# Attention followed by a gated MLP on one core: weights converted in PSUM without POOL, layer norm's scaling on ACT, v's remainder on VectorE, and the first batch's product with v divided by the sums

## The chip, the core and the metric

The kernel runs on one core of one Trainium2 chip. The metric is the device time of one execution in microseconds (us). The engines are called as in the profile: PE (matrix products; PEld its weight loads), DVE (VectorE), ACT (ScalarE), POOL (GpSimd) and SP, which issues the DMAs.

## The reference

There are 4 batches of 768 tokens. Attention has 8 heads of 64; each token sees 8 global tokens and the last 96 tokens, with a bias that falls with the distance. Its output, 512 wide, goes through an MLP whose second half of hidden units is normalised, mixed over the tokens and multiplied with the first half.

```python
scores = scale * np.matmul(q, k.transpose(0, 1, 3, 2))
scores = np.where(keep, scores + bias[None], -1000000000.0)
scores = scores - np.max(scores, axis=-1, keepdims=True)
a = np.exp(scores)
a = a / (np.sum(a, axis=-1, keepdims=True) + 1e-09)
x = np.matmul(a, v)                       # then (batch, token, 512)
h = np.maximum(x @ w_in, 0.0)
u, v = h[..., :512], h[..., 512:]
v_n = (v - mean(v)) / np.sqrt(var(v) + 1e-06)
v_s = np.einsum('ts,bsd->btd', w_spatial, v_n) + b_spatial[None, :, None]
out = (u * v_s) @ w_out
```

The inputs q, k, v and w_spatial are fp32. The weights w_in and w_out come as 64-bit floats.

## The kernel before, in words

**Blocks.** A batch has 6 blocks of 128 tokens; n counts the 24 blocks of all batches. Block n needs only its own keys and those of the block before it, with the global keys copied over the first columns of the older one. For a block, `prep` loads q and k, `prep_v` loads v, `scores` makes the probabilities and `values` the product with v.

**Scores.** PE multiplies (L364 in batch 0, L367 in the others) into PSUM tiles of two heads. On DVE, L373 adds the bias and takes the row maximum; on ACT, L377 makes the exponentials and, by an accumulator, their sums `sm`. L259 and L260 (function `recip`, DVE) add 1e-9 to the sums of four heads and take the reciprocals `rc`; then L388 on POOL multiplies each head's probabilities with its reciprocal.

**Values.** PE transposes the probabilities (L421), ACT brings them out of PSUM, and PE multiplies with v (L430 in batch 0, L451 in the others). The result x is kept as two parts, a rounded `xth` (ACT) and a remainder `xtl` (DVE or POOL); L123 and L127 are the helpers that write any such pair. In batch 0 this is done on halves of 64 partitions straight out of PSUM. The branch for `folded(n)` exists but is not taken, since `CFG["fold"]` is empty: there the probabilities stay undivided, the reciprocals of all 8 heads are spread over 512 columns (`rows`, a buffer shared with the q input of later batches), transposed by PE and copied by ACT to `div` (shared with the k input), and the product with v is multiplied with them.

**Batch 0 and the rest.** Batch 0 multiplies q with k and probabilities with v in plain fp32. The other batches split q, k, v and the probabilities into a rounded part and a remainder; v's split is on POOL (L129 the rounded part, L123 the remainder), and the split q and k are copied by 12 DMAs a block (L300 to L303).

**Weights.** `split_weights` turns a 128x512 piece of 64-bit weights into a rounded part and a remainder. There are 8 pieces of w_in and 4 of w_out. One ACT operation (L222) makes the absolute values, six DVE operations (L223 to L228) assemble the fp32 number and its low part, ACT rounds (L50), and POOL subtracts and adds (L230, L231). All tiles are in SBUF. The fp32 spatial weights are split on ACT and POOL (`w_t_h`, `w_t_l`, 128x768, six of them).

**MLP.** `mlp_v` (L493 on PE) computes a block's second half of hidden units; ACT applies the relu, DVE takes mean and variance (L499, L500), POOL computes (var + 1e-6)^-0.5 (L501, L502), DVE scales (L503), and ACT and POOL split the result into `vnh` and `vnl`. `mlp_u` (L516) computes the first half for 256 tokens, `mlp_s` (L531) mixes over the tokens, and `mlp_o` (L549) multiplies with w_out. Each takes its PSUM tiles from the pool `ps_m`, which has two buffers.

**Order.** The lists `S` (batch 0) and `T` (the others) in `CFG` give the order of the steps in the program: P is `prep`, S `scores`, W `prep_v`, A `values`; V, U, G, O are the MLP steps with their lag in batches and their block; I and Q convert w_in and w_out, T the spatial weights. A scheduler with a timeline model then reorders the instructions of each engine. So each engine has one queue, worked off in order, and what stands in it is fixed before the run. The letters after `CFG` keys such as `vhi` name the engine of an operation: a for ACT, v for DVE, p for POOL.

Of the kernel before, what the change touches and what calls it, by code (L numbers as in the profile page):

```python
# [30 lines left out]
def attn_then_spatial_gating_kernel(  # L31
# [173 lines left out]
    def split_weights(src, hi, lo, key=None):  # L205
        w = src.shape[-1]
        if src.dtype == F32:
            st = work.tile([P, w], F32, name="wst", tag="u", bufs=3)
# [13 lines left out]
        nc.scalar.activation(m, upper.bitcast(F32), AF.Abs)  # L222
        nc.vector.tensor_scalar(out=c, in0=upper.bitcast(F32), scalar1=UPPER_MAX, scalar2=-UPPER_MAX, op0=ALU.min, op1=ALU.max)  # L223
        nc.vector.tensor_scalar(out=ai, in0=ci, scalar1=3, scalar2=0x3FFFFFFF, op0=ALU.logical_shift_left, op1=ALU.bitwise_and)
        nc.vector.scalar_tensor_tensor(out=ai, in0=ci, scalar=-0x40000000, in1=ai, op0=ALU.bitwise_and, op1=ALU.bitwise_or)
        nc.vector.scalar_tensor_tensor(out=a, in0=m, scalar=UPPER_MIN, in1=a, op0=ALU.is_ge, op1=ALU.mult)
        nc.vector.tensor_scalar(out=ci, in0=ai, scalar1=-0x800000, scalar2=None, op0=ALU.bitwise_and)
        nc.vector.scalar_tensor_tensor(out=m, in0=lower.bitcast(U32), scalar=2.0 ** -52, in1=c, op0=ALU.mult, op1=ALU.mult)  # L228
# [1 line left out]
        E("wsub").tensor_tensor(out=a, in0=a, in1=hi.bitcast(F32), op=ALU.subtract)  # L230
        E("wadd").tensor_tensor(out=lo, in0=a, in1=m, op=ALU.add)  # L231
# [26 lines left out]
    def recip(out, sums):
        nc.vector.tensor_scalar(out=out, in0=sums, scalar1=1e-9, scalar2=None, op0=ALU.add)  # L259
        nc.vector.reciprocal(out=out, in_=out)  # L260
# [80 lines left out]
    def scores(n, qq):  # L341
# [14 lines left out]
        rc = work.tile([P, H], F32, name="rc", bufs=2)
        W = P if i == 0 else 2 * P
        probs = []
        for g in range(NP):
# [8 lines left out]
            for j in range(2):  # L368
# [8 lines left out]
                nc.scalar.activation(pr, pr, AF.Exp, bias=mn[:, h:h + 1], scale=-1.0, accum_out=sm[:, h:h + 1])  # L377
# [109 lines left out]
    def mlp_v(b, i):  # L487
# [14 lines left out]
        nc.gpsimd.tensor_tensor(out=rs, in0=rs, in1=nhalf, op=ALU.pow)  # L502
        nc.vector.tensor_scalar(out=vr, in0=vr, scalar1=mv[:, 0:1], scalar2=rs, op0=ALU.subtract, op1=ALU.mult)  # L503
# [238 lines left out]
```

## Time and profile before

| | |
|---|---|
| median of 3 runs | 530.93 us (529.34 to 532.43) |
| profiled execution | 530.32 us |
| span of its instructions | 528.5 us |
| mean granted clock of PE | 0.970 |
| PE busy | 474.2 us (90%), weight loads 427.9 us (81%) |
| DVE busy | 350.6 us (66%), 972 instructions |
| POOL busy | 325.4 us (62%), 450 instructions |
| ACT busy | 301.9 us (57%), 800 instructions |

The span is 1.8 us shorter than the profiled execution's time. The busy times are sums over the whole span, and the stages differ, so a share says little about any one of them. A group of instructions is shown by line, engine, operation, written tile, read tiles, shape and count, with the busy time, the mean in ns, and the engine's idle time just before. In the timeline a row starts with the start and the duration in us. Chains and waits are inferred from semaphores.

### The profile page before, as it was taken

Reading aid. Unit: us, or ns where it says so; the run is one execution under the profiler, and the core shown is the slowest. Engines: PE = TensorE matmul, PEld = TensorE weight load, DVE = VectorE, ACT = ScalarE, POOL = GpSimd, SP = SyncE. Lnnn points to the kernel's source line nnn. Section 1 sums busy time; section 2 is a strip of 40 time slices with the busy share of each in tenths; the row PEclk is TensorE's granted clock in tenths of the full one; section 3 lists DMA queues with packets and bytes.
Section 4 is the critical chain, followed back from the end, with each engine's and each line's share of the span. In section 5 each row is a group of like instructions: output and inputs, shape, how many; then the busy total and the mean of one; then the engine's idle time right before and its main releaser. Section 6 shows DMA issues by size and latency. Waiting matters only on the chain.

```text
span 528.5 us, 9830 instructions
## 1 busy us (share of the span) xinstructions
PE 474.2 (90%) x3116; PEld 427.9 (81%) x3116; DVE 350.6 (66%) x972; ACT 301.9 (57%) x800; POOL 325.4 (62%) x450
## 2 busy tenths in 40 slices
PE   3757599898988999997989999989999999979994
PEld 2535489678977999986979899969989899869994
DVE  6899988869697585476785775767587856331210
ACT  3775478666666484666575575675475576431111
POOL 6999997866774753846662947644753757523320
PEclk9987789999999999999999999998999999989998
DMA  7993412961755755466655764655755760000002
GB/s 173 288 245 106 144 60 52 214 145 51 153 139 138 172 133 125 98 154 160 145 118 150 169 163 99 147 146 137 159 112 147 183 140 21 22 20 1 21 35 73
DMA packets 68269, 65.50 MB, mean 124 GB/s; under 512 B 6672, under 2 KB 49936, under 8 KB 68208
## 3 DMA queue, kind: packets, MB, share of 16 engines
q1 hardware_dynamic: 68208, 64.78, 49.9%
q8 instruction: 27, 0.44, 0.4%
q14 instruction: 34, 0.28, 0.2%
HBM read 29.76 MB, written 6.68 MB: 69 GB/s over the span
## 4 chain that ended last, share of the span: by engine, by line
PE 48%; DVE 17%; DMA 13%; SPq 8%; ACT 6%; issue 5%; POOL 2%; DVEq 0%; ACTq 0%; POOLq 0%
PE sps L531 13%; PE vps L493 8%; PE ups L516 8%; PE ops L549 7%; PE ops L451 4%; DVE pr L373 3%; PE pt L421 3%; DMA qkraw<-in_k_dram 3%; PE sp L367 3%; ACT pr L377 2%; DMA qkraw<-in_q_dram 2%; DMA kring<-qkraw 2%; SPq L303 2%; DVE qkraw L123 2%; SPq L300 2%
## 5 line engine op out<-in xcount | busy, mean ns | idle before, releaser
L388 POOL TENSOR_SCALAR pr<-pr,rc 128x256 f32<-128x256 f32 (+1 forms) x192 | 99.6, 537 | 23.4 <-DVE rc L260 9.1
L377 ACT ACTIVATE pr<-pr,mn 128x256 f32<-128x256 f32 (+1 forms) x192 | 92.2, 482 | 33.7 <-DVE mn L373 32.5
L421 PE MATMUL pt<-ident,pr 128*128 128x128 f32 x352 | 58.4, 280 | 14.7 <-POOL pr L388 11.6
L373 DVE CUSTOM_DVE_ANT_0 pr<-sp,bias 128x256 f32<-128x256 f32 (+1 forms) x192 | 68.1, 395 | 4.6 <-PE sp L364 1.4
L421 PEld LDWEIGHTS pt<-ident,pr 128*128 128x128 f32 x352 | 42.0, 143 | 23.9 <-POOL pr L388 16.5
L123 DVE TENSOR_TENSOR pth<-pt,pth 128x512 fp32r<-128x512 f32 (+1 forms) x72 | 46.0, 642 | 16.6 <-ACT pth L127 15.4
L535 POOL TENSOR_TENSOR g<-g,u 128x512 f32<-128x512 f32 x24 | 32.0, 1331 | 34.8 <-DVE g L533 34.7
L127 ACT ACTIVATE pth<-pt 128x512 fp32r<-128x512 f32 (+1 forms) x72 | 39.2, 558 | 23.6 <-PE pt L421 20.9
L123 POOL TENSOR_TENSOR xtl<-c,xth 128x256 fp32r<-128x256 f32 x36 | 27.3, 758 | 35.8 <-ACT xth L127 28.5
L123 POOL TENSOR_TENSOR vnl<-vr,vnh 128x512 fp32r<-128x512 f32 x24 | 31.9, 1332 | 27.6 <-ACT vnh L127 26.6
L531 PE MATMUL sps<-w_t_l,vnh 128*128 128x256 f32 x288 | 45.8, 286 | 0.0
L531 PE MATMUL sps<-w_t_h,vnh 128*128 128x256 f32 x288 | 44.9, 286 | 0.8 <-ACT u L517 0.5
L451 PE MATMUL ops<-pth,vring 128*128 128x256 f32 x264 | 41.8, 288 | 3.0 <-DVE pth L123 2.1
L461 DVE TENSOR_TENSOR c<-ops,c 64x256 f32<-64x256 f32 x72 | 30.3, 421 | 21.4 <-ACT c L50 16.6
L531 PE MATMUL sps<-w_t_h,vnl 128*128 128x256 f32 x288 | 44.4, 285 | 0.0
L364 PE MATMUL sp<-kring,q 128*128 128x256 f32 (+1 forms) x96 | 28.7, 450 | 16.8 <-DMA kring<-in_k_dram 9.9
L451 PEld LDWEIGHTS ops<-pth,vring 128*128 128x128 f32 x264 | 36.4, 192 | 5.2 <-DVE pth L123 2.8
L367 PE MATMUL sp<-kring,q 128*128 128x256 f32 (+1 forms) x144 | 38.3, 292 | 2.4 <-DMA q<-qkhi 1.2
L531 PEld LDWEIGHTS sps<-w_t_h,vnh 128*128 128x128 f32 x288 | 38.7, 191 | 1.6 <-ACT vnh L127 0.8
L531 PEld LDWEIGHTS sps<-w_t_l,vnh 128*128 128x128 f32 x288 | 39.0, 191 | 0.0
L533 DVE TENSOR_TENSOR g<-sps,b_bc 128x512 f32<-128x512 f32 x24 | 16.5, 686 | 33.8 <-PE sps L531 31.5
L531 PEld LDWEIGHTS sps<-w_t_h,vnl 128*128 128x128 f32 x288 | 38.6, 191 | 0.0
(115 smaller groups left out, 1204.4 us busy)
## 6 DMA issues: line engine op xcount, KB each, us to landing
q<-qkhi SPq DMA_DIRECT2D x72, 128.0 KB, 2.5
ql<-qkraw SPq DMA_DIRECT2D x72, 128.0 KB, 2.5
out_dram<-o SPq DMA_DIRECT2D x23, 256.0 KB, 2.6
qkraw<-in_q_dram SPq DMA_DIRECT2D x36, 128.0 KB, 3.0
qkraw<-in_k_dram SPq DMA_DIRECT2D x36, 128.0 KB, 2.9
raw<-in_v_dram SPq DMA_DIRECT2D x18, 256.0 KB, 3.2
kring<-qkhi SPq DMA_DIRECT2D x36, 128.0 KB, 2.5
kring<-qkraw SPq DMA_DIRECT2D x36, 128.0 KB, 2.5
```

Of the source, the lines that this page charges most:

```text
L123: e_lo.tensor_tensor(out=lo, in0=src, in1=hi.bitcast(F32), op=ALU.subtract)
L127: nc.scalar.activation(hi, src, AF.Copy)
L367: nc.tensor.matmul(sp[:, j], lhsT=a[:, g, j] if CFG["dup"] else a[:, h], rhs=kring[:, h, sl], start=(y == 0), stop=(y == 1))
L373: nc.vector.tensor_tensor_reduce(out=pr, in0=sp[:, j], in1=bt, scale=-scale, scalar=3e38, op0=ALU.add, op1=ALU.min, accum_out=mn[:, h:h + 1],)
L377: nc.scalar.activation(pr, pr, AF.Exp, bias=mn[:, h:h + 1], scale=-1.0, accum_out=sm[:, h:h + 1])
L388: nc.gpsimd.tensor_scalar(out=pr, in0=pr, scalar1=rc[:, h:h + 1], scalar2=1.0, op0=ALU.mult, op1=ALU.mult)
L421: nc.tensor.transpose(pt[:, c, j], probs[2 * g + j][:, c * P:(c + 1) * P], ident)
L451: nc.tensor.matmul(ops[:, j], lhsT=vring[:, order[c], g, 2 * j:2 * j + 2].rearrange("p x d -> p (x d)"), rhs=pth[:, 2 * c + j].rearrange(" ...
L493: nc.tensor.matmul(ps, lhsT=a[:, t, toks], rhs=w[:, t, FH:], start=(x == 0), stop=(x == len(passes) - 1))
L516: nc.tensor.matmul(ps[:, j], lhsT=w[:, t, f * P:(f + 1) * P], rhs=a[:, t], start=(x == 0), stop=(x == len(passes) - 1))
L531: nc.tensor.matmul(ps[:, j], lhsT=vn[b, s][x][:, f * P:(f + 1) * P], rhs=w[:, s, ts_], start=(y == 0), stop=(y == len(passes) - 1))
L549: nc.tensor.matmul(ps[:, cs], lhsT=a[:, f, x * P:(x + 1) * P], rhs=w[:, f, cs], start=(y == 0), stop=(y == len(passes) - 1))
```

## The change

Five things change, all by `CFG` and the code behind it.

- `wp`: `split_weights` keeps its working number `wx` in a PSUM tile of `ps_m`, computes in place, and does the last subtraction and sum on DVE. ACT's two operations stay.
- `fold` is `'0'`: batch 0 takes the folded branch. The 48 products on POOL go; per block come one `rows` copy on POOL, 4 transposes on PE, one `div` copy on ACT, 4 products on DVE (64x256), and the split of x on 128 partitions in two ACT and two DVE operations instead of four and four.
- `vhi`, `vlo`: v's rounded part moves from POOL to ACT, its remainder from POOL to DVE.
- `vrn`: the layer norm's scaling moves from DVE to ACT as scale and bias per row; POOL computes the bias, minus mean times scale, by two more operations on one column.
- `bias1`, `bias2`: the 16 scalings that make the bias tables move from POOL to ACT.

The sums now lie in two tiles whose second column holds 1e-9, and `recip` adds the pair with a reduction instead of adding a constant; in batch 0 it is called once per block.

```diff
-CFG = {... 'bias1': 'pppppppp', 'bias2': 'pppppppp', ... 'vhi': 'p', 'vlo': 'p', ... 'fold': '', ...}
+CFG = {... 'bias1': 'aaaaaaaa', 'bias2': 'aaaaaaaa', ... 'vhi': 'a', 'vlo': 'v', ... 'wp': 1, 'vrn': 'a', ... 'fold': '0', ...}
...
+        if CFG["wp"]:
+            x = ps_m.tile([P, w], F32, name="wx", tag="m")
+            xi = x.bitcast(I32)
+            a = work.tile([P, w], F32, name="wa", tag="vnl", bufs=6)
+            m = work.tile([P, w], F32, name="wm", tag="ev", bufs=nb("ev"))
+            ai = a.bitcast(I32)
+            nc.scalar.activation(m, upper.bitcast(F32), AF.Abs)
+            nc.vector.tensor_scalar(out=x, in0=upper.bitcast(F32), scalar1=UPPER_MAX, scalar2=-UPPER_MAX, op0=ALU.min, op1=ALU.max)
+            nc.vector.tensor_scalar(out=ai, in0=xi, scalar1=3, scalar2=0x3FFFFFFF, op0=ALU.logical_shift_left, op1=ALU.bitwise_and)
+            nc.vector.scalar_tensor_tensor(out=xi, in0=xi, scalar=-0x40000000, in1=ai, op0=ALU.bitwise_and, op1=ALU.bitwise_or)
+            nc.vector.scalar_tensor_tensor(out=x, in0=m, scalar=UPPER_MIN, in1=x, op0=ALU.is_ge, op1=ALU.mult)
+            nc.vector.tensor_scalar(out=ai, in0=xi, scalar1=-0x800000, scalar2=None, op0=ALU.bitwise_and)
+            nc.vector.scalar_tensor_tensor(out=m, in0=lower.bitcast(U32), scalar=2.0 ** -52, in1=a, op0=ALU.mult, op1=ALU.mult)
+            cp(E("whi"), hi, x)
+            nc.vector.tensor_tensor(out=x, in0=x, in1=hi.bitcast(F32), op=ALU.subtract)
+            nc.vector.tensor_tensor(out=lo, in0=x, in1=m, op=ALU.add)
+            return
...
+    sums = [pers.tile([P, H, 2], F32, name=f"sums{x}") for x in range(2)]
+    for x in range(2):
+        nc.vector.memset(sums[x], 1e-9)
     def recip(out, sums):
-        nc.vector.tensor_scalar(out=out, in0=sums, scalar1=1e-9, scalar2=None, op0=ALU.add)
+        nc.vector.tensor_reduce(out=out, in_=sums, op=ALU.add, axis=mybir.AxisListType.X)
         nc.vector.reciprocal(out=out, in_=out)
...
-        sm = work.tile([P, H], F32, name="sm", bufs=2)
+        sm = sums[n % 2]
...
-                nc.scalar.activation(pr, pr, AF.Exp, bias=mn[:, h:h + 1], scale=-1.0, accum_out=sm[:, h:h + 1])
+                nc.scalar.activation(pr, pr, AF.Exp, bias=mn[:, h:h + 1], scale=-1.0, accum_out=sm[:, h, 0:1])
...
-        nc.vector.tensor_scalar(out=vr, in0=vr, scalar1=mv[:, 0:1], scalar2=rs, op0=ALU.subtract, op1=ALU.mult)
+        if CFG["vrn"] == "a":
+            sh = work.tile([P, 1], F32, name="sh", bufs=2)
+            nc.gpsimd.tensor_tensor(out=sh, in0=mv[:, 0:1], in1=rs, op=ALU.mult)
+            nc.gpsimd.tensor_scalar(out=sh, in0=sh, scalar1=-1.0, scalar2=1.0, op0=ALU.mult, op1=ALU.mult)
+            nc.scalar.activation(vr, vr, AF.Identity, bias=sh, scale=rs)
+        else:
+            nc.vector.tensor_scalar(out=vr, in0=vr, scalar1=mv[:, 0:1], scalar2=rs, op0=ALU.subtract, op1=ALU.mult)
```

The scheduler makes a new order out of this on every engine. Three places follow; lines of the changed kernel are larger by 18 to 28.

On POOL, the beginning of batch 0 before: the probabilities' products (L388), the weights' subtraction and sum (L230, L231) and the spatial weights' remainders (L123) alternate.

```order
L388 TENSOR_SCALAR pr<-pr,rc 128x128 x4
L230 TENSOR_TENSOR wa<-wa,w_in_h 128x512
L388 TENSOR_SCALAR pr<-pr,rc 128x128 x4
L231 TENSOR_TENSOR w_in_l<-wa,wm 128x512
L265 TENSOR_SCALAR kring_114<-kg 128x4x32
L123 TENSOR_TENSOR w_t_l<-wst_493,w_t_h 128x768
L230 TENSOR_TENSOR wa<-wa,w_in_h 128x512
L388 TENSOR_SCALAR pr<-pr,rc 128x256 x4
L123 TENSOR_TENSOR w_t_l<-wst_497,w_t_h 128x768
```

The same place now, where `rows` are the spread reciprocals of a block:

```order
L54 TENSOR_SCALAR rows<-rc 128x512
L123 TENSOR_TENSOR w_t_l<-wst_479,w_t_h 128x768
L123 TENSOR_TENSOR w_t_l<-wst_483,w_t_h 128x768
L287 TENSOR_SCALAR kring_118<-kg 128x4x32
L123 TENSOR_TENSOR w_t_l<-wst_824,w_t_h 128x768
L123 TENSOR_TENSOR w_t_l<-wst_871,w_t_h 128x768
L54 TENSOR_SCALAR rows<-rc 128x512
```

Only the spatial weights' remainders, the global keys (`kg`) and the new copies are left there.

On DVE, the first two pieces of w_out before: the conversion runs through the six operations, with a remainder of x between.

```order
L223 TENSOR_SCALAR wc<-wst 128x512 x2
L259 TENSOR_SCALAR rc<-sm 128x4
L260 RECIPROCAL rc<-rc 128x4
L224 TENSOR_SCALAR wa<-wc 128x512 x2
L225 SCALAR_TENSOR_TENSOR wa<-wc,wa 128x512 x2
L226 SCALAR_TENSOR_TENSOR wa<-wm,wa 128x512 x2
L227 TENSOR_SCALAR wc<-wa 128x512
L123 TENSOR_TENSOR xtl<-ops,xth 64x2x128
```

The end of the same two pieces now. `wx` is the tile in PSUM, `xs` the divided product, and `qkraw` the input of batch 1's first block.

```order
L229 SCALAR_TENSOR_TENSOR wx<-wm,wx 128x512
L282 RECIPROCAL rc<-rc 128x8
L462 TENSOR_TENSOR xs<-ops,div 64x256
L229 SCALAR_TENSOR_TENSOR wx<-wm,wx 128x512
L462 TENSOR_TENSOR xs<-ops,div 64x256
L230 TENSOR_SCALAR wa<-wx 128x512 x2
L231 SCALAR_TENSOR_TENSOR wm<-wst,wa 128x512 x2
L233 TENSOR_TENSOR wx<-wx,w_out_h 128x512 x2
L234 TENSOR_TENSOR w_out_l<-wx,wm 128x512 x2
L123 TENSOR_TENSOR qkraw<-qkraw,qkhi 128x512 x2
L123 TENSOR_TENSOR xtl<-xs,xth 128x2x128 x2
```

Both pieces hold a buffer of `ps_m` until L234, and the remainders of q and k for batch 1 come behind them; before, those stood far ahead, in the middle of batch 0.

On SP, the loads of q and k for batch 1's first block (`qkraw`) before, among the loads of the first weights:

```order
L244 DMA wst_493<-in_moe_w_spatial_dram 128x768
L244 DMA wst_497<-in_moe_w_spatial_dram 128x768
L248 DMA b_bc<-in_moe_b_spatial_dram 128x768
L294 DMA qkraw<-in_q_dram 64x4x128
L197 DMA wst<-in_moe_w_in_dram 128x1024
L294 DMA qkraw<-in_q_dram 64x4x128
L294 DMA qkraw<-in_k_dram 64x4x128 x2
```

And now:

```order
L197 DMA wst<-in_moe_w_out_dram 128x1024 x2
L502 DMA vring_218<-in_v_dram 32x512
L347 DMA vring_218<-in_v_dram 128x512
L502 DMA vring_218<-in_v_dram 32x512
L316 DMA qkraw<-in_k_dram 64x4x128
L316 DMA qkraw<-in_q_dram 64x4x128 x2
L316 DMA qkraw<-in_k_dram 64x4x128
```

They have moved behind all loads of w_in and the first two of w_out.

More of the change, by code (lines that the diff above doesn't have):

```diff
@@ L24 @@
 NGMAX = 32
-CFG = {'bpos': 1, 'v0pos': 0, 'bias1': 'pppppppp', 'bias2': 'pppppppp', 'S': [['P', 'I01', 'S', 'W', 'A', 'I00'], ['P', 'S', 'W', 'T01', 'T00', 'A', 'V00', 'B00'], ['P', 'S', 'V01', 'Q00', 'Q01', 'W', 'U00', 'A'], ['V02', 'P', 'W', 'T04', 'S', 'T03', 'A'], ['P', 'S', 'W', 'A'], ['P', 'A', 'T02', 'Q02', 'V04', 'V03', 'S', 'W', 'Q03', 'T05', 'U01']], 'T': [['P', 'W', 'A', 'V15', 'U12', 'S'], ['P', 'A', 'S', 'G10', 'W'], ['P', 'W', 'A', 'S', 'O10', 'V00'], ['G11', 'P', 'A', 'S', 'V01', 'O11', 'W'], ['P', 'W', 'A', 'U00', 'G12', 'V02', 'S'], ['P', 'W', 'U01', 'A', 'S', 'V03', 'V04', 'O12']], 'END': ['V15', 'U12'], 'lead': {}, 'pre_n': 1, 'pre0': 0, 'pre1': 1, 'whi': 'a', 'wsub': 'p', 'wadd': 'p', 'wth': 'a', 'wtl': 'p', 'vhi': 'p', 'vlo': 'p', 'qhi': 'a', 'qlo': 'v', 'khi': 'a', 'klo': 'v', 'pth0': 'aaaa', 'x0h': 'aa', 'x0l': 'vv', 'pth': 'aaaa', 'xh': 'aa', 'c1': 'aa', 'xl': 'pppp', 'vnh': 'a', 'vnl': 'p', 'gm': 'pp', 'gh': 'aa', 'gl': 'pv', 'o': 'aa', 'norm0': 'pppppppp', 'norm': 'pppppppp', 'dup': 1, 'fold': '', 'xb': 1, 'div': 'a', 'rows': 'p', 'xf0h': 'a', 'xf0l': 'v', 'xdiv': 'v', 'xbh': 'a', 'xbl': 'p', 'b_rawqk': 1, 'b_ev': 3, 'b_raw': 1, 'b_pr': 10, 'b_pth': 2, 'b_c1': 3, 'b_ps_s': 2, 'b_ps_p': 2, 'b_ps_o': 2, 'b_ps_m': 2}
@@ new lines @@
+CFG = {'bpos': 1, 'v0pos': 0, 'bias1': 'aaaaaaaa', 'bias2': 'aaaaaaaa', 'S': [['P', 'I01', 'S', 'W', 'A', 'I00'], ['P', 'S', 'W', 'T01', 'T00', 'A', 'V00', 'B00'], ['P', 'S', 'V01', 'Q00', 'Q01', 'W', 'U00', 'A'], ['V02', 'P', 'W', 'T04', 'S', 'T03', 'A'], ['P', 'S', 'W', 'A'], ['P', 'A', 'T02', 'Q02', 'V04', 'V03', 'S', 'W', 'Q03', 'T05', 'U01']], 'T': [['P', 'W', 'A', 'V15', 'U12', 'S'], ['P', 'A', 'S', 'G10', 'W'], ['P', 'W', 'A', 'S', 'O10', 'V00'], ['G11', 'P', 'A', 'S', 'V01', 'O11', 'W'], ['P', 'W', 'A', 'U00', 'G12', 'V02', 'S'], ['P', 'W', 'U01', 'A', 'S', 'V03', 'V04', 'O12']], 'END': ['V15', 'U12'], 'lead': {}, 'pre_n': 1, 'pre0': 0, 'pre1': 1, 'whi': 'a', 'wsub': 'p', 'wadd': 'p', 'wth': 'a', 'wtl': 'p', 'vhi': 'a', 'vlo': 'v', 'qhi': 'a', 'qlo': 'v', 'khi': 'a', 'klo': 'v', 'pth0': 'aaaa', 'x0h': 'aa', 'x0l': 'vv', 'pth': 'aaaa', 'xh': 'aa', 'c1': 'aa', 'xl': 'pppp', 'vnh': 'a', 'vnl': 'p', 'gm': 'pp', 'gh': 'aa', 'gl': 'pv', 'o': 'aa', 'norm0': 'pppppppp', 'norm': 'pppppppp', 'wp': 1, 'vrn': 'a', 'dup': 1, 'fold': '0', 'xb': 1, 'div': 'a', 'rows': 'p', 'xf0h': 'a', 'xf0l': 'v', 'xdiv': 'v', 'xbh': 'a', 'xbl': 'p', 'b_rawqk': 1, 'b_ev': 3, 'b_raw': 1, 'b_pr': 10, 'b_pth': 2, 'b_c1': 3, 'b_ps_s': 2, 'b_ps_p': 2, 'b_ps_o': 2, 'b_ps_m': 2}
```

## The prediction

> **What bounds the kernel now.** The page's busy shares are averages over unlike stages, so the first view I read after it is the table of busy time by stretch. Per stretch it gives length, then busy us (instructions) of PE, PE's weight loads, DVE, ACT and POOL, then the granted clock and the DMA share.
>
> ```profile
> 10.00:66.00 56.00, 36.76 (x134) 26.56 (x134) 53.10 (x131) 35.60 (x102) 55.50 (x61) 0.85 0.75 198
> 66.00:84.00 18.00, 17.73 (x94) 15.74 (x95) 13.86 (x37) 13.31 (x36) 16.35 (x25) 0.91 0.27 75
> 84.00:137.40 53.40, 48.74 (x309) 43.28 (x308) 45.59 (x118) 36.71 (x100) 40.11 (x49) 1.00 0.50 115
> 137.40:466.00 328.60, 315.98 (x2216) 291.27 (x2215) 223.59 (x635) 203.51 (x544) 193.99 (x291) 0.99 0.55 132
> ```
>
> I cut at 137.4 because the first spatial product of batch 0 (L531) starts there, and by program order it follows everything that the change touches in batch 0. From then on PE is busy 316.0 of 328.6 us: 12.6 us is nearly all that the other engines can give back there. Before it PE is idle or slow while DVE (53.1 of 56.0) and POOL (55.5 of 56.0) are both full. So the change is decided in the front part, 0 to 137.4 us, and the question is which of the two full engines is the bound. The timeline answers it: two executions of L225, the first at its undisturbed length, with a one-source operation behind it.
>
> ```profile
> 41.42 0.68 DVE L225 SCALAR_TENSOR_TENSOR wa<-wc,wa 128x512 int32<-128x512 int32 x1
> 42.02 0.41 DVE L224 TENSOR_SCALAR wa<-wc 128x512 int32<-128x512 int32 x1
> ...
> 44.30 2.31 DVE L225 SCALAR_TENSOR_TENSOR wa<-wc,wa 128x512 int32<-128x512 int32 x1
> ```
>
> ```profile
> 43.79 2.28 POOL L123 TENSOR_TENSOR w_t_l<-wst,w_t_h 128x768 fp32r<-128x768 f32 x1
> ```
>
> The same operation takes 0.68 us, or 2.31 us if it starts inside a two-input operation of POOL, and it ends when that one does. DVE's full load is therefore partly waiting on POOL, and the groups of the front part show how much (count, busy us, mean ns, idle before).
>
> ```profile
> L373 DVE CUSTOM_DVE_ANT_0 pr<-sp,bias 128x256 f32<-128x256 f32 (+1 forms) x64 | 22.3, 383 | 3.0 <-PE sp L364 1.4 <-PE pt L421 1.2
> L228 DVE SCALAR_TENSOR_TENSOR wm<-wst,wc 128x512 f32<-128x512 uint32 x12 | 15.0, 1258 | 0.2
> L225 DVE SCALAR_TENSOR_TENSOR wa<-wc,wa 128x512 int32<-128x512 int32 x12 | 14.0, 1176 | 0.0
> L226 DVE SCALAR_TENSOR_TENSOR wa<-wm,wa 128x512 f32<-128x512 f32 x12 | 11.4, 952 | 0.4 <-ACT wm L222 0.3
> L123 DVE TENSOR_TENSOR xtl<-ops,xth 64x256 fp32r<-64x256 f32 x24 | 10.1, 419 | 6.4 <-ACT xth L127 6.1
> L227 DVE TENSOR_SCALAR wc<-wa 128x512 int32<-128x512 int32 x12 | 8.8, 733 | 0.1
> L224 DVE TENSOR_SCALAR wa<-wc 128x512 int32<-128x512 int32 x12 | 7.6, 642 | 0.1
> L223 DVE TENSOR_SCALAR wc<-wst 128x512 f32<-128x512 f32 x12 | 6.9, 582 | 0.6 <-DMA wst<-in_moe_w_in_dram 0.6
> L259 DVE TENSOR_SCALAR rc<-sm 128x4 f32<-128x4 f32 x16 | 6.0, 376 | 1.7 <-ACT pr L377 1.7
> ```
>
> The weights take 15.0+14.0+11.4+8.8+7.6+6.9 = 63.7 us of DVE. At 0.68 for two inputs and 0.41 for one they would take 12 x (3 x 0.68 + 3 x 0.41) = 39.2, so about 24 us is contention. POOL's groups of the same stretch:
>
> ```profile
> L388 POOL TENSOR_SCALAR pr<-pr,rc 128x256 f32<-128x256 f32 (+1 forms) x60 | 38.9, 664 | 3.7 <-DVE rc L260 2.9 <-PE ops L430 0.6
> L230 POOL TENSOR_TENSOR wa<-wa,w_in_h 128x512 f32<-128x512 f32 x8 | 12.4, 1549 | 0.0
> L123 POOL TENSOR_TENSOR w_t_l<-wst,w_t_h 128x768 fp32r<-128x768 f32 x6 | 12.4, 2063 | 0.0
> L231 POOL TENSOR_TENSOR w_in_l<-wa,wm 128x512 fp32r<-128x512 f32 x8 | 11.7, 1460 | 0.0
> ```
>
> **The front part, edit by edit.** On POOL the change takes out the 48 products of batch 0 (about 48 x 0.664 = 32 us), the weights' subtraction and sum (24.1 us for w_in, the same again per piece for w_out) and the bias, and adds six copies of one input. POOL stops being full; that by itself gives nothing as long as DVE sets the pace. So I balance DVE. For PSUM operands at 512 columns, and for the rest of the sum, I use these rows of the back part:
>
> ```profile
> L533 DVE TENSOR_TENSOR g<-sps,b_bc 128x512 f32<-128x512 f32 x24 | 16.5, 686 | 33.8 <-PE sps L531 31.5 <-POOL gl L123 2.2
> L259 DVE TENSOR_SCALAR rc<-sm 128x4 f32<-128x4 f32 x33 | 16.4, 497 | 15.3 <-ACT pr L377 15.0
> ...
> L503 DVE TENSOR_SCALAR vr<-vr,mv,rs 128x512 f32<-128x512 f32 x19 | 10.9, 571 | 10.6 <-POOL rs L502 10.5
> ```
>
> Weights: eight operations a piece in place of six. Five have two inputs, 0.68 each with or without PSUM (L225, L533). Three have one source and touch PSUM, which no row shows: between 0.41 (L224, both sides in SBUF) and 0.686 (L533, one side in PSUM). I take 0.69, the row with PSUM: 12 x (5 x 0.68 + 3 x 0.69) = 65.6 us, against 55.6 with the other end. Each operation starts about 0.08 before its forerunner ends (41.42 + 0.68 against 42.02), so 24 more of them give back 1.9. Net 65.6 - 63.7 - 1.9 = 0, or -10 at the low end. The contention is thus removed and spent again: two more operations, and three slower ones. The Trainium skill, in VectorE: DVE Perf Modes, section "Why PSUM operands drop a tier", says that an fp32 operation with a PSUM operand runs at one element a cycle, where a one-source operation in SBUF runs at two; by it the sum is the upper one, by the SBUF row it is 10 us lower, and no row here shows such an operation.
>
> What is left of POOL's two-input work, six w_t_l of 2.06 us, can still stretch the two-SBUF operations: 0 to 6 us, I take +2. Sums: 16 calls of L259 become ten reductions, of unknown price between nothing and today's 0.376: -6.0 to -2.2, I take -4. Product with v divided: 24 multiplications of the form of xtl (0.419) are added, +10.1; the 24 subtractions of xtl (-10.1) become twelve at double the partitions and the same columns, +5.0; net +5. Three remainders of v fall before 137.4: +2.0. Five scalings of L503 leave: -2.9. DVE's sum: 0 + 2 - 4 + 5 + 2 - 2.9 = **+2 us**.
>
> So the gain has to come out of DVE's waits. From 10 us on DVE is idle 2.9 + 4.1 + 7.8 = 14.8 us in the front part. 6.1 of this is xtl waiting for ACT's xth (its row above), which goes from 24 halves to twelve wholes with operations of other blocks between; and POOL ends last in one stretch of the chain of waits (start, length, what):
>
> ```profile
> 93.72 1.89 POOL wa L230 x2
> ...
> 98.32 1.27 POOL w_out_l L231
> ```
>
> From 93.72 to 99.59 the program stands on POOL's last weights; now no POOL operation lies there. I count 6 of the 14.8 us as gone and leave 9. Front part: +2 - 6 = **-4 us**. ACT takes the bias (no row shows it there; at most 16 x 0.664, the price of L388's like work on a disturbed POOL, so up to 11 us) and six copies of the reciprocals out of PSUM, while it is busy 35.6 of 56.0: hidden by DVE's load; if that cover is gone, part of the 11. PE gets 24 transposes more, hidden as long as DVE is the bound.
>
> **The back part.** PE's waits after 125 us, and what v's split costs POOL (ns min/median/max):
>
> ```profile
> PE pt L421 <- POOL pr L388: 4.4, 3, 2.3
> ```
>
> ```profile
> L129 POOL TENSOR_SCALAR vring<-raw x16: 612/618/1116, 145.3 to 427.4; 128x512 fp32r<-128x512 f32 x16
> L123 POOL TENSOR_TENSOR vring<-raw,vring x16: 1268/1292/1610, 146.0 to 428.1; 128x512 fp32r<-128x512 f32 x16
> ```
>
> POOL loses 16 x 1.91 = 30.6 of its 194.0 us and gets two one-column operations per layer norm. Half of PE's 4.4 us should go: -2. DVE swaps 18 scalings (-10.3) for 16 remainders (+10.9) and gets cheaper sums (up to -16.4): off the path. ACT gets 16 + 18 operations of about 0.62, +21 us on 203.5 of 328.6: hidden, 0 to +4. The layer norm's longer way (POOL twice more, then ACT) is waited for a batch later, and at the end of the program it lies beside the product with the input weights. The back part gives **-2 us**.
>
> The profiled execution took 530.32 us, 528.5 of it span; the median of the runs is 530.93. 530.3 - 4 - 2 = **524 us**.
>
> **Rivals.** (1) No change: the first block of batch 1 starts later and eats the front's gain. Its q and k use the buffers that now hold the reciprocals' rows and their transposes, so its loads can't be issued before the last block of batch 0 has been transposed; before they were issued from 18 us on.
>
> ```profile
> 18.07 0.54 SPq L294 DMA_DIRECT2D qkraw<-in_q_dram  x1
> ```
>
> ```profile
> 87.47 0.16 DVE L259 TENSOR_SCALAR rc<-sm 128x4 f32<-128x4 f32 x1
> ```
>
> ```profile
> 99.39 0.41 PE L367 MATMUL sp<-kring,q 128*128 128x128 f32 x1
> ```
>
> ```profile
> 245.75 0.58 SPq L294
> 246.32 0.05 issue
> 246.37 2.93 DMA qkraw<-in_q_dram
> ```
>
> From the last sums of batch 0 (87.47) to the first scores of batch 1 (99.39) it takes 11.9 us now. The new way is: rows 0.62, four transposes 0.6 as an estimate, issue 0.58, load 2.93, ACT's and DVE's split 0.62 and 0.68 (the first taken from POOL's one-input row), twelve issues of 0.58, landing 2.93 as for the load, so 15.9 us: +4, which cancels the front's -4. For it: nothing shortens these transfers. Against it: DVE and PE have the last weights and batch 0's products to do meanwhile. Time 528.5 to 531.
>
> (2) Slower: the two PSUM buffers of ps_m. Two pieces of w_out hold both from their first operation to their last, and batch 0's products with w_in queue behind them on PE. The chain gives their pace:
>
> ```profile
> 210.92 2.75 PE vps L493 x12
> 214.61 2.86 PE ups L516 x24
> ```
>
> After the pair PE has 144 ups and 48 vps left, 144 x 0.12 + 48 x 0.23 = 28 us, and some 12 us of attention: 40 us. DVE, which starts on the scores at 9 us, has by its order ten pieces (48 us), 48 scores (48 x 0.383 = 18), the divisions and remainders of four and a half blocks (10) and 2 us of contention ahead: 87, with 7 of the waits 94, which gives 134 for the first spatial product. It decides from 97 us on: then the front part is longer than now. Writing to PSUM is not shown; 0.2 us more for the four operations a piece that do it is 10 x 4 x 0.2 = 8 us, so 101, and no gain on POOL's chain: 530 + 7 = **537 us**.
>
> (3) A larger gain: one-source operations on PSUM stay near 0.41, DVE loses 8 to 10 us and its waits go with them: 524 - 10 = 514, down to 511 with the rest of PE's waits.
>
> **How the numbers follow.** Forecast (517 to 528) 0.45; no change 0.22; slower 0.18; larger gain 0.15. About 0.5% (2.7 us) is what a measurement of this kernel can tell from no change. Faster 0.45 + 0.15 = 0.60, same 0.22, slower 0.18. The range of 511 to 537 takes in the low end of the PSUM price and the slower case up to its own number.
>
> **What would show it.** Right: no DVE operation of the weights over 1 us except beside w_t_l; the three one-source ones near 0.69; DVE's busy time from 10 us to the first spatial product about 115 us where the three stretches now hold 112.6, POOL's under half of its 112.0; that product near 134. Wrong: this product after 137 with PE waiting for a DVE operation on wx (rival 2) or for DMAs of q (rival 1), or one-source operations on PSUM at 0.45 (rival 3). A stretch after the front part that differs by over 5 us would break the last step.

## The result, and the profile after

The changed kernel is slower: a median of 538.43 us (536.92 to 539.50, 4 runs) against 531.19 (529.34 to 532.43, 4 runs), a ratio of 1.0137 with a 95% interval of 1.0098 to 1.0176. Ratios here leave out runs over 1.5% above the fastest of the same kernel, and medians are of all runs; the two part only in e5 below. The profiled execution took 539.5 us, with a span of 537.7 and a granted clock of 0.946.

First the table of busy time by stretch, cut again where the first spatial product (now L559) starts; columns as in the prediction.

```profile
10.00:66.00 56.00, 38.93 (x161) 30.15 (x160) 52.55 (x144) 41.36 (x123) 13.96 (x12) 0.85 0.67 193
66.00:84.00 18.00, 17.21 (x83) 14.59 (x84) 14.98 (x42) 11.82 (x31) 3.93 (x8) 0.91 0.16 50
84.00:151.98 67.98, 56.49 (x327) 49.44 (x326) 46.98 (x128) 40.62 (x104) 21.30 (x45) 0.87 0.52 130
151.98:537.70 385.72, 368.30 (x2566) 337.81 (x2565) 221.61 (x641) 232.70 (x593) 186.29 (x302) 0.97 0.44 112
```

That product starts at 151.98 us where it started at 137.43: the front part is 14.6 us longer, the rest 5.4 shorter (385.7 against 528.5 - 137.4 = 391.1). To 84 us the stretches are like those of before, with POOL at a quarter of its load; the whole loss is behind 84 us. There PE is idle for 11.5 of 68.0 us, and its clock is 0.87 where it was 1.00. The groups of VectorE up to that product:

```profile
L462 DVE TENSOR_TENSOR xs<-ops,div 64x256 f32<-64x256 f32 x24 | 10.0, 415 | 4.8 <-ACT div L50 3.7 <-PE ops L452 0.9
L231 DVE SCALAR_TENSOR_TENSOR wm<-wst,wa 128x512 f32<-128x512 uint32 x12 | 9.2, 773 | 0.1
L228 DVE SCALAR_TENSOR_TENSOR wx<-wx,wa 128x512 int32<-128x512 int32 x12 | 8.3, 691 | 0.1
L226 DVE TENSOR_SCALAR wx<-wst 128x512 f32<-128x512 f32 x12 | 8.3, 688 | 1.0 <-DMA wst<-in_moe_w_in_dram 0.9
...
L230 DVE TENSOR_SCALAR wa<-wx 128x512 int32<-128x512 int32 x12 | 8.1, 686 | 0.1
L227 DVE TENSOR_SCALAR wa<-wx 128x512 int32<-128x512 int32 x12 | 8.1, 681 | 0.1
L123 DVE TENSOR_TENSOR xtl<-xs,xth 128x256 fp32r<-128x256 f32 x12 | 6.3, 535 | 8.2 <-ACT xth L127 8.1
...
L281 DVE TENSOR_REDUCE rc<-sums 128x8 f32<-128x16 f32 (+1 forms) x10 | 1.6, 159 | 0.1
```

The stretching is nearly gone (means of 681 to 773 ns, up to 1258 before), and the one-source operations on PSUM take 0.68 to 0.69 us, all as forecast. By the Trainium skill, VectorE: DVE Perf Modes, section "Why PSUM operands drop a tier", an fp32 operation with a PSUM operand runs at one element a cycle; the trace agrees. VectorE's work is not the loss: 52.55 + 14.98 + 46.98 = 114.5 us from 10 us on, 112.6 before. The loss is when it is done. Here is the timeline of VectorE around the first two pieces of w_out, Q00 and Q01:

```profile
77.59 0.68 DVE L226 TENSOR_SCALAR wx<-wst 128x512 f32<-128x512 f32 x1
...
83.85 0.69 DVE L226 TENSOR_SCALAR wx<-wst 128x512 f32<-128x512 f32 x1
...
89.65 1.29 DVE L227 TENSOR_SCALAR wa<-wx 128x512 int32<-128x512 int32 x2
...
98.24 1.28 DVE L234 TENSOR_TENSOR w_out_l<-wx,wm 128x512 fp32r<-128x512 f32 x2
99.70 1.29 DVE L123 TENSOR_TENSOR qkraw<-qkraw,qkhi 128x512 fp32r<-128x512 f32 x2 [0.18 <-ACT qkhi L127]
106.75 0.76 DVE L123 TENSOR_TENSOR xtl<-xs,xth 128x256 fp32r<-128x256 f32 x2 [5.76 <-ACT xth L127]
```

The first operation of each piece takes a PSUM buffer at 77.6 and 83.9 us, and the last gives it back at about 98.9 and 99.5: 21 and 16 us for the 11 us of work that the two take together, since scores and products stand between them. Then the timeline of PE: the first product of U00 (the products `ups` of batch 0's first 256 tokens) in the kernel before, and, of the changed kernel, from that product to the operation behind the last of U00:

```profile
77.87 0.82 PE L516 MATMUL ups<-xth,w_in_h 128*128 128x256 f32 x4
```

```profile
99.14 1.20 PE L544 MATMUL ups<-xth,w_in_h 128*128 128x256 f32 x4
...
105.61 0.59 PE L452 MATMUL ops<-pth,vring 128*128 128x256 f32 x2
```

U00, which started at 77.87 us in the kernel before and went in small groups into PE's gaps, now starts right behind the pair and runs as one block of 48 products. Meanwhile VectorE gets no scores and no products of v. It idles 5.76 us up to 106.75, waiting for ACT's xth, which stands in ACT's order behind the two relus of U00 (at 102.99 and 105.81 us). The busy times show it, and what came behind it (ten and then four microseconds each):

```profile
100.00:110.00 10.00, 10.00 (x70) 9.32 (x69) 1.75 (x4) 2.43 (x6) 0.00 (x0) 0.96 0.71 159
```

```profile
96.00:100.00 4.00, 3.43 (x12) 2.97 (x13) 3.81 (x7) 2.51 (x5) 0.00 (x0) 0.50 0.42 121
...
124.00:128.00 4.00, 2.08 (x8) 1.68 (x8) 4.00 (x9) 2.87 (x7) 3.20 (x7) 0.58 0.81 198
128.00:132.00 4.00, 3.25 (x15) 3.25 (x16) 3.87 (x10) 3.56 (x7) 0.80 (x4) 0.50 0.61 146
```

From 100 to 110 us VectorE does 1.75 us of work; from 120 to 136 it is full, and up to 129 us PE waits for it. PE's longest wait of this part, 4.32 us, ends at 125.92, and its clock is 0.58 and 0.50 in the stretches around and behind that. The other two pieces of w_out hold the buffers in the same way, each from its first operation (112.72 and 124.87 us) to its last (128.70 and 144.40), and the two later blocks of `ups` start only then:

```profile
128.75 1.22 PE L544 MATMUL ups<-xth,w_in_h 128*128 128x256 f32 x4 [0.75 <-DVE w_out_l L234]
...
144.45 0.74 PE L544 MATMUL ups<-xth,w_in_h 128*128 128x256 f32 x4 [0.58 <-DVE w_out_l L234]
```

The first spatial product follows the second of them. PE's recorded waits for these buffers are short, 0.75 and 0.58 us, and ahead of U00 there is none: in PE's order it stands behind transposes that start at 98.43 us. The waits of PE up to the first spatial product (us in total, times, longest), after, and then the row of before whose place the wait for rows has taken:

```profile
PE rps L435 <- POOL rows L54: 13.3, 5, 5.1
PE sp L386 <- DMA kring<-in_k_dram: 9.8, 2, 8.1
PE ops L473 <- DVE pth L123: 4.3, 1, 4.3
```

```profile
PE pt L421 <- POOL pr L388: 7.2, 6, 4.9
```

And the group of the 24 transposes that the division adds on PE:

```profile
L435 PE MATMUL rps<-ident,rows 128*128 128x128 f32 x24 | 5.7, 382 | 13.3 <-POOL rows L54 13.3
```

Seen from PE, the 9.2 us of span are 8.6 us more busy time (482.8 against 474.2) and 0.6 us more idle time (54.9 against 54.3). 5.7 of the 8.6 are these transposes; the other 2.9 come with a lower clock (0.946 against 0.970), which is argued and not separated by a run.

### The profile page after: what moved, and what is told of

The parts are those of the page before. It is cut to its first block, busy times and chain, and to the rows that moved or that the text cites. A ratio compares the mean times of both kernels' runs of the same rounds, so it can differ in the third digit from the quotient of the medians.

```text
span 537.7 us, 9854 instructions
## 1 busy us (share of the span) xinstructions
PE 482.8 (90%) x3140; PEld 433.9 (81%) x3140; DVE 341.3 (63%) x992; ACT 328.3 (61%) x852; POOL 230.0 (43%) x380
## 4 chain that ended last, share of the span: by engine, by line
PE 55%; DMA 14%; DVE 13%; ACT 7%; SPq 6%; issue 3%; POOL 1%; ACTq 0%; POOLq 0%; DVEq 0%
PE sps L559 14%; PE ups L544 10%; PE vps L515 8%; PE ops L577 8%; PE pt L443 5%; PE ops L473 4%; PE sp L389 4%; DMA kring<-qkraw 4%; DMA qkraw<-in_k_dram 3%; DMA wst<-in_moe_w_in_dram 2%; DVE pr L395 2%; DMA qkraw<-in_q_dram 2%; ACT pr L399 2%; PE ops L452 1%; SPq L322 1%
## 5 line engine op out<-in xcount | busy, mean ns | idle before, releaser
L410 POOL TENSOR_SCALAR pr<-pr,rc 128x256 f32<-128x256 f32 (+1 forms) x144 | 67.6, 489 | 29.2 <-DVE rc L282 9.7
L395 DVE CUSTOM_DVE_ANT_0 pr<-sp,bias 128x256 f32<-128x256 f32 (+1 forms) x192 | 68.8, 395 | 15.7 <-PE sp L389 12.1
L443 PE MATMUL pt<-ident,pr 128*128 128x128 f32 x352 | 63.0, 293 | 2.0 <-POOL pr L410 1.6
L123 DVE TENSOR_TENSOR pth<-pt,pth 128x512 fp32r<-128x512 f32 (+1 forms) x72 | 46.0, 644 | 20.4 <-ACT pth L127 19.2
L123 POOL TENSOR_TENSOR xtl<-c,xth 128x256 fp32r<-128x256 f32 x36 | 28.5, 790 | 68.8 <-ACT xth L127 67.6
L443 PEld LDWEIGHTS pt<-ident,pr 128*128 128x128 f32 x352 | 46.1, 151 | 9.8 <-POOL pr L410 3.7
L473 PE MATMUL ops<-pth,vring 128*128 128x256 f32 x264 | 44.2, 297 | 6.2 <-DVE pth L123 4.3
L473 PEld LDWEIGHTS ops<-pth,vring 128*128 128x128 f32 x264 | 37.8, 197 | 9.5 <-DVE pth L123 4.7
L559 PE MATMUL sps<-w_t_h,vnh 128*128 128x256 f32 x288 | 44.1, 282 | 1.1 <-ACT u L545 1.1
L559 PE MATMUL sps<-w_t_l,vnh 128*128 128x256 f32 x288 | 43.8, 281 | 0.0
L559 PE MATMUL sps<-w_t_h,vnl 128*128 128x256 f32 x288 | 43.1, 280 | 0.0
L389 PE MATMUL sp<-kring,q 128*128 128x256 f32 (+1 forms) x144 | 37.8, 292 | 4.7 <-DMA q<-qkhi 3.4
L123 DVE TENSOR_TENSOR qkraw<-qkraw,qkhi 128x512 fp32r<-128x512 f32 x36 | 26.9, 755 | 21.0 <-ACT qkhi L127 17.4
L123 POOL TENSOR_TENSOR vnl<-vr,vnh 128x512 fp32r<-128x512 f32 x24 | 31.2, 1306 | 20.7 <-ACT vnh L127 20.7
L559 PEld LDWEIGHTS sps<-w_t_h,vnh 128*128 128x128 f32 x288 | 37.9, 188 | 1.7 <-ACT u L545 1.3
L127 ACT ACTIVATE qkhi<-qkraw 128x512 fp32r<-128x512 f32 x36 | 22.6, 629 | 25.1 <-DMA qkraw<-in_q_dram 16.8
L386 PE MATMUL sp<-kring,q 128*128 128x256 f32 (+1 forms) x96 | 25.4, 409 | 13.7 <-DMA kring<-in_k_dram 9.8
L559 PEld LDWEIGHTS sps<-w_t_l,vnh 128*128 128x128 f32 x288 | 37.6, 188 | 0.0
```

The lines of the kernel that those rows point to most:

```text
L123: e_lo.tensor_tensor(out=lo, in0=src, in1=hi.bitcast(F32), op=ALU.subtract)
L127: nc.scalar.activation(hi, src, AF.Copy)
L389: nc.tensor.matmul(sp[:, j], lhsT=a[:, g, j] if CFG["dup"] else a[:, h], rhs=kring[:, h, sl], start=(y == 0), stop=(y == 1))
L395: nc.vector.tensor_tensor_reduce(out=pr, in0=sp[:, j], in1=bt, scale=-scale, scalar=3e38, op0=ALU.add, op1=ALU.min, accum_out=mn[:, h:h + 1],)
L410: nc.gpsimd.tensor_scalar(out=pr, in0=pr, scalar1=rc[:, h:h + 1], scalar2=1.0, op0=ALU.mult, op1=ALU.mult)
L443: nc.tensor.transpose(pt[:, c, j], probs[2 * g + j][:, c * P:(c + 1) * P], ident)
```

## The experiments

Three theories were set against each other. B: two pieces of w_out hold both PSUM buffers of ps_m, and U00 queues behind them (rival 2). L: the first loads of q and k of batch 1 come late (rival 1). R: PE waits for the rows of reciprocals ahead of work that does not need them. Later two more: P, the price of operations on PSUM, and F, the added transposes. All results in one table; U00 is the start of its first product, "by 220" the number of products that PE has started by 220 us (of 3140, without the division of 3116), and span, PE busy and PE idle (their difference) are of the profiled execution, all in us.

| kernel | median | ratio to before (95%) | U00 | by 220 | span | PE busy | PE idle |
|---|---|---|---|---|---|---|---|
| kernel before | 531.19 | 1 | 77.9 | 1115 | 528.5 | 474.2 | 54.3 |
| changed kernel | 538.43 | 1.0137 (1.0098 to 1.0176) | 99.1 | 1069 | 537.7 | 482.8 | 54.9 |
| e1 rows in other buffers | 543.90 | 1.0234 (1.0188 to 1.0280) | 102.6 | 1074 | 537.2 | 475.8 | 61.4 |
| e2 wx in SBUF | 531.66 | 0.9985 (0.9956 to 1.0015) | 60.0 | 1131 | 531.9 | 480.9 | 51.0 |
| e3 w_out's wx in SBUF | 531.88 | 1.0012 (0.9988 to 1.0036) | 81.9 | 1155 | 526.7 | 476.4 | 50.3 |
| e4 no division | 545.68 | 1.0273 (1.0194 to 1.0353) | 106.9 | 987 | 542.0 | 479.6 | 62.4 |
| e5 U00 ahead | 537.85 | 1.0072 (1.0025 to 1.0118) | 83.5 | 1119 | 534.5 | 478.4 | 56.1 |
| e6 e3, no division | 530.14 | 0.9987 (0.9952 to 1.0023) | 81.5 | 1106 | 527.6 | 471.4 | 56.2 |
| e7 old weights, no division | 533.08 | 1.0030 (0.9991 to 1.0069) | 74.7 | 1040 | 534.1 | 477.9 | 56.2 |
| e8 before + division | 540.03 | 1.0183 (1.0115 to 1.0251) | 65.6 | 1114 | 537.0 | 480.0 | 57.0 |
| e9 rows late | 539.79 | 1.0139 (1.0101 to 1.0177) | 106.2 | 1075 | 535.4 | 475.3 | 60.1 |
| e10 e3, rows late | 528.50 | 0.9923 (0.9892 to 0.9953) | 88.5 | 1153 | 528.1 | 476.0 | 52.1 |
| e11 e2, rows late | 535.71 | 1.0039 (1.0011 to 1.0067) | 68.8 | 1148 | 535.8 | 479.1 | 56.7 |
| e12 old weights, rows late | 527.97 | 0.9903 (0.9864 to 0.9941) | 67.1 | 1153 | 528.3 | 472.2 | 56.1 |
| e13 buffers held only | 536.02 | 1.0113 (1.0088 to 1.0138) | 99.9 | 1075 | 534.4 | 478.4 | 56.0 |
| e14 first pair in SBUF | 529.82 | 0.9998 (0.9975 to 1.0021) | 82.3 | 1141 | 527.0 | 475.5 | 51.5 |
| e15 second pair in SBUF | 538.45 | 1.0145 (1.0099 to 1.0191) | 98.3 | 1138 | 536.4 | 480.4 | 56.0 |
| e16 e8, rows late | 536.33 | 1.0109 (1.0066 to 1.0153) | 67.5 | 1132 | 536.0 | 479.9 | 56.1 |

The column "by 220" tells early losses from late ones, which the start of U00 alone does not: the changed kernel, e1, e4, e9 and e13 have fallen behind there, while e11, e15 and e16, which are slow too, have not; they lose their time later. It does not name a cause: e7 has fallen behind too, with no buffer held.

**e1.** The rows and their transposes leave the buffers of q and k.

```diff
-            rows = work.tile([P, H, D], F32, name="rows", tag="raw0", bufs=1)
+            rows = work.tile([P, H, D], F32, name="rows", tag="rawh0", bufs=1)
-            div = work.tile([P, NP, P], F32, name="div", tag="raw1", bufs=1)
+            div = work.tile([P, NP, P], F32, name="div", tag="rawh1", bufs=1)
```

> The changed kernel, with the rows of reciprocals and their transposes in the buffers of qkhi (needed only after a load has landed) in place of the buffers into which q and k of the first block of batch 1 are loaded, so that these loads no longer wait. Theory L (those loads, issued from 107 us in place of 18 us, make the front part longer): 531 to 534 us, the q load before 90 us and the first spatial product near 146. Theory B (the second PSUM buffer pair, held by the weights' pieces of w_out, is what holds U00 on the tensor engine to 99.5 us): U00 stays near 99 and the time at 536 to 540. Theory R (the fold's rows, 13.3 us of the tensor engine's waits): 536 to 540 too.

The issue of the first load of q, of the changed kernel and then of e1:

```profile
95.09 1.22 SPq L316 DMA_DIRECT2D qkraw<-in_q_dram  x2
```

```profile
17.25 1.20 SPq L316 DMA_DIRECT2D qkraw<-in_q_dram  x2
```

The load is back at 17 us and the time is no better: PE reaches the scores of batch 1 at 108.69 us, at 109.62 in the changed kernel, since U00 stands ahead of them in both. L is not the cause; e3 below, whose loads come later still, says the same. Why e1 is 5.5 us above the changed kernel, and above all three ranges, is open; its U00 comes 3.4 us later still.

**e2 and e3.** wx in SBUF, for all pieces and for those of w_out.

```diff
-            x = ps_m.tile([P, w], F32, name="wx", tag="m")
+            x = work.tile([P, w], F32, name="wx", tag="vnh", bufs=6)   # e3: only for w_out
```

> The changed kernel, with the weights' working tile wx in SBUF (the buffers that wc had before) in place of PSUM; the eight operations a piece on VectorE stay. Theory B (buffers held): U00 starts by 85 us, the first spatial product comes at 137 or earlier, 521 to 528 us, the one-source operations at 0.41 us giving 12 x 3 x 0.28 = 10 us of VectorE on top. Theory L: the loads stay late, 533 to 537. Theory R: the tensor engine's wait for rows stays near 13 us, 530 to 535.

> The changed kernel, with wx in SBUF for the four pieces of w_out alone; the eight pieces of w_in keep PSUM. Theory B: nearly all of the loss goes, since only w_out's pieces stood in front of U00: 527 to 532 us. Theories L and R: only the price of 12 cheaper one-source operations on VectorE, 3 us at most, 535 to 538.

The first product of U00 in e3:

```profile
81.89 0.63 PE L544 MATMUL ups<-xth,w_in_h 128*128 128x256 f32 x4
```

Both are back at the kernel before: e3 at the edge of B's range, e2 3.7 us above B's and inside R's, though its wait for rows fell to 2.6 us, which R had at 13. The 10 us of VectorE that the price was thought to be are not there: all operations of the weights together take VectorE 66.5 us in the changed kernel, 67.2 in e2 and 65.4 in e3. In SBUF the one-source operations are again longer than 0.41 us on average (L226, L227 and L230 in e2: 453, 643 and 729 ns).

**e4.** The division undone in the changed kernel.

```diff
-'fold': '0'
+'fold': ''
```

> The changed kernel without the division of batch 0's products: POOL scales the 48 products again, as before; the weights stay in PSUM, and the rest of the change stays. Theory R: the tensor engine's wait for rows (13.3 us) goes, POOL's scaling costs less back since POOL has no weights: 528 to 532 us. Theory B: U00 still stands behind w_out's pieces, 535 to 542. Theory L: q and k load early again, 531 to 534.

Slower by 7 us, and above B's range too, so the division is not what lost the time here, and R falls in this form. U00 comes at 106.9, and now PE's wait for the buffer stands right ahead of it, where the changed kernel has none:

```profile
106.91 1.22 PE L544 MATMUL ups<-xth,w_in_h 128*128 128x256 f32 x4 [5.27 <-DVE w_out_l L234]
```

**e5.** The table's third row, `'V01', 'Q00', 'Q01', 'W', 'U00', 'A'`, becomes `'V01', 'U00', 'Q00', 'Q01', 'W', 'A'`.

> The changed kernel with one entry of the order's table moved: U00 stands ahead of Q00 and Q01, so that it takes its PSUM buffers before the pieces of w_out do. Every operation and every buffer is as in the changed kernel. Theory B (the buffers are held): U00 starts near 82 us and the time is that of the run with w_out's tile in SBUF, 530 to 534 us. Theory P (what helped there was the price of the 12 one-source operations, 0.69 us against 0.41): 536 to 540.

Between the two by the ratio (about 535 us), while the median lies in P's range. U00 starts at 83.5, but the wait has moved to the next that needs a buffer, the products vps (waits of PE from 84 to 160 us):

```profile
PE vps L515 <- DVE w_out_l L234: 3.1, 1, 3.1
```

**e6 and e7.** e6 is e3 with `'fold': ''`; e7 is the changed kernel with `'wp': 0` and `'fold': ''`.

> wx of w_out's pieces in SBUF, and POOL scales batch 0's 48 products again. Theory F (the fold's 24 transposes are 5 us of work on the tensor engine, which is busy nine tenths of the time, so nothing hides them): 525 to 529 us against 531.9 with the fold. Theory G (the fold takes more waits off the front part than it adds work, as the 7 us between the changed kernel and the one without the fold say): 535 to 540.

> The changed kernel with the weights converted as before (POOL subtracts and adds, SBUF) and without the fold: the bias on ACT, v's split on ACT and VectorE, the layer norm's scaling on ACT and the sums by one reduction are left. Forecast by the back part's gain of 5.3 us in the changed kernel: 524 to 528 us. If that gain was only work moved ahead of the cut at the first spatial product: 529 to 533.

e6 lies between the two ranges and ends within the measurement of e3: in the two profiled executions the division removes 5.9 us of PE's idle time (56.2 to 50.3) and adds 5.0 of busy time. e7 gains nothing (the upper end of its second range); the 5.4 us of the back part were not a gain of these moves by themselves.

**e8.** The kernel before with `'fold': '0'`.

> The kernel before with the division of batch 0's products alone; all else is as before. Theory F: the transposes' 5 us come on top, 534 to 538 us. Theory G: POOL, full in the front part there, loses 48 scalings, and the time falls to 523 to 528.

9 us slower, more than F's 5; the weights on POOL are untouched and U00 comes at 65.6, so this loss has nothing to do with B. Part of it comes after 220 us.

**e9 to e12.** The rows' transposes move in the order of a block. e9 does this alone, e10 on e3, e11 on e2, e12 with `'wp': 0`.

```diff
-        if folded(n):
-            rps = ps_p.tile([P, NP, P], F32, name="rps", tag="p")
...
             if whole(n):
...
+                if folded(n) and g == 1:
+                    rps = ps_p.tile([P, NP, P], F32, name="rps", tag="p")
...
                 if g % 2:
                     if folded(n):
```

> The changed kernel with the four transposes of the reciprocals' rows moved, in the order of a block, from ahead of its eight transposes of probabilities to just ahead of the first product that needs them; the weights stay in PSUM. Theory R (the tensor engine's 13.3 us of waiting for rows stands ahead of transposes that need no rows): most of that wait goes, the idle time of the tensor engine falls from 54.9 to 45 to 48 us, 528 to 532 us. Theory B (the late U00 decides whatever the waits ahead of it): 536 to 540.

> wx of w_out's pieces in SBUF and the rows' transposes late. Theories R and B each take a part: 10.8 us of waiting for rows are left where only w_out's tile is in SBUF (531.9 us), two thirds of it should go: 522 to 527. If that wait is only the tensor engine being ahead of VectorE, it comes back as another wait: 530 to 533.

> wx in SBUF for all twelve pieces and the rows' transposes late. With rows transposed first there were only 2.6 us of waiting for rows in the run with wx in SBUF (531.7 us), so theory R gives 529 to 532. A theory by VectorE's load (24 more one-source operations at 0.41 in place of 0.69, 6.7 us less than with only w_out's tile in SBUF) gives 522 to 526.

> The weights converted as before (POOL subtracts and adds), the fold with its rows late, the other moves kept. Tells what the conversion in PSUM is worth by itself: if POOL's two-input work beside VectorE (24 us of stretching before) is what matters, 533 to 538; if VectorE's total is the same either way, as the prediction's sum has it, 526 to 531.

In e9 PE's wait for rows up to 84 us, and U00:

```profile
PE rps L452 <- POOL rows L54: 1.2, 1, 1.2
```

```profile
106.23 1.22 PE L543 MATMUL ups<-xth,w_in_h 128*128 128x256 f32 x4 [1.29 <-DVE w_out_l L234]
```

The wait is gone and the time is the same, in B's range. But PE's idle time rose to 60.1 us in place of falling to 45 to 48, and U00 comes 7.1 us later still, so that nothing ahead of a late U00 counts is B's reading and not shown by this run. Without the held buffers the wait counts some: e10, between its two ranges, is 3.4 us below e3 and faster than the kernel before. e11 is worse than e2 and fits no theory. e12, with POOL in the weights again, is as fast as e10 and in its second range: by itself the conversion without POOL is worth nothing that these runs show. e10 and e12 are faster than both kernels.

**e13 to e15.** e13 is e3 with an empty tile of ps_m beside each piece of w_out; e14 and e15 are e3 for two of the four pieces.

```diff
+            if key[0] == "o":
+                hold = ps_m.tile([P, w], F32, name="hold", tag="m")
+                nc.vector.memset(hold[:, 0:1], 0.0)
...
             nc.vector.tensor_tensor(out=lo, in0=x, in1=m, op=ALU.add)
+            if key[0] == "o":
+                nc.vector.tensor_copy(out=a[:, 0:1], in_=hold[:, 0:1])
```

> wx of w_out's pieces in SBUF (531.9 us by itself), and beside each piece an empty PSUM tile out of the same two buffers, with one column set before the piece's first VectorE operation and read after its last: the buffers are held as in the changed kernel, and every one of the eight operations works in SBUF. Theory B (the holding): U00 near 99 us and 536 to 540 us, as the changed kernel. Theory P (the price): 532 to 533.

> wx in SBUF for the first two pieces of w_out alone (Q00 and Q01, which stand ahead of U00). Theory B: 531 to 534 us, as with all four. Theory P: half of the gain of 6.5, 535 to 536.

> wx in SBUF for the last two pieces of w_out alone (Q02 and Q03, which stand behind U00). Theory B: U00 stays near 99 us and the time at 536 to 539. Theory P: 535 to 536, the same as with the first two.

The timelines of VectorE and PE in e13:

```profile
79.86 0.06 DVE L223 MEMSET hold<- 128x1 f32 x1
...
86.02 0.06 DVE L223 MEMSET hold<- 128x1 f32 x1
...
99.73 0.16 DVE L239 COPY wa<-hold 128x1 f32<-128x1 f32 x1
```

```profile
99.94 0.74 PE L549 MATMUL ups<-xth,w_in_h 128*128 128x256 f32 x4
```

U00 starts 0.05 us after the first empty tile is read, and the time is 1.0113 of the kernel before with every weight operation of w_out in SBUF, where e3 without the empty tiles has 1.0012 and the changed kernel 1.0137: the holding alone makes most of the loss. It makes it in the same place, too: by 220 us PE has started 1075 products, in the changed kernel 1069 and in e3 1155. The order of all engines changes with this edit as with every other. U00 in e14 and in e15:

```profile
82.27 0.63 PE L544 MATMUL ups<-xth,w_in_h 128*128 128x256 f32 x4
```

```profile
98.32 1.20 PE L544 MATMUL ups<-xth,w_in_h 128*128 128x256 f32 x4
```

With the first pair out of PSUM the loss is gone (1 us under B's range). With the second pair out the time is that of the changed kernel, as B said, but it is not the same loss:

```profile
138.61 0.74 PE L559 MATMUL sps<-w_t_h,vnh 128*128 128x256 f32 x5
```

Although U00 starts at 98.32, the first spatial product of e15 comes 13.4 us earlier than in the changed kernel, and by 220 us PE has started 1138 products, nearly as many as in e14 (1141). It falls behind only then: from 240 to 260 us PE is busy for 16.3 us at a clock of 0.75, in e14 for 17.8 at 0.91; why is open. So e15 does not show that the first pair alone makes the loss; in e14 and e15, with one pair each in the buffers, the early loss is not there. B is shown for the holding of ps_m's buffers by the pieces of w_out as a whole (e13 against e3); no run gave ps_m a third buffer. P is out: the weights take VectorE 65.4 us in e3, 66.2 in e13, 65.8 in e14 and 66.9 in e15, 1.5 us apart at most, where the times lie up to 9 us apart.

**e16.** e8 with its rows late.

> The kernel before with the fold alone, its rows transposed just ahead of their first use. The fold alone with rows first was 540.0 us. If the place of the rows was its cost: 528 to 532. If the 24 transposes and the products on VectorE are: 536 to 540.

At the lower end of its second range. By the medians the place of the rows was 3.7 us, though the intervals of e8 and e16 overlap, and 6 us stay, near F's 5. Why the division costs 6 us there and yet gains 5 from e7 to e12 is open: every edit reorders all engines, and no run here separates that.

## Why the prediction was wrong, point by point

- **The weights' price on VectorE.** Right: 0.68 to 0.69 us for one source on PSUM, stretching left in one of the weights' groups only (L231, 773 ns; the remainders xtl took 535 ns where 419 were counted), and a sum of +2 that came out as 114.5 - 112.6 = +1.9. One reading of the lines is off, and nothing hangs on it: the stretched L225 ends at 46.61 us, 0.54 us after POOL's operation and not with it. The reductions cost 0.159 us each, near the low end; small.
- **VectorE's waits.** This is the step that failed: "I count 6 of the 14.8 us as gone and leave 9." They are 142.0 - 114.5 = 27.5 us. Of these, xtl's wait for xth, which was to shrink from 6.1, is 8.1. The ground for the 6 was that POOL's last weights, to 99.59 us, had left the chain. They had, but VectorE ends the same pair at 99.5. And a pair that ends then was harmless only while it lay in SBUF: now it holds both buffers that U00 needs, and e13 shows that the holding makes most of the loss.
- **Rival 2** has the mechanism that happened: the two buffers, U00 behind them, a pair that ends after 97 us. That its price of 7 us meets the 7.2 measured is luck: its 94 and 8 are 102 and not 101, 5 us past 97, which does not give 7, and the 8 us for writing to PSUM did not occur (0.68 to 0.69 us an operation). Its own sum let the pair end at 94 without them, and so it got 0.18. From 9 to 99.5 us VectorE worked 82.0 us where 78 were counted (the division's products and remainders took 13.1, not 10), and it waited 8.6 where 7 were. The loss also took another form than that sum: from the end of the pair to the first spatial product it counted 40 us, and they were 52.5. The 48 products of U00 came as one block, VectorE ran dry, PE's clock fell, and the second pair, which the sum leaves out, held up the next two blocks.
- **The transposes on PE**, "hidden as long as DVE is the bound". Put at nothing without a row that shows it: PE is busy nine tenths of the span, and the transposes are 3.7 to 5.7 us of that in the runs with the division (e12 and the changed kernel; e3 4.8). What they cost in time is not settled: e8 and e16 lose 9 and 6 us with the division, while e3 ends as e6 and e12 below e7.
- **The back part.** Forecast -2, measured -5.4, more than double; the direction holds, but e7 shows no gain from its moves alone.
- **Rival 1.** Its mechanism is there (the first load issued at 95.09 us), its price is not: e3 issues that load at 106.27, later still, and loses nothing.
- **Rival 3** did not occur.

The range ended at 537, the rival's own number, with nothing for the error of that number.
